# A planner's transfer latency, a row split of one load, and one planner dependency in an attention–mixing–FFN kernel

## Chip, cores and metric

The kernel runs on one core of a Trainium2 chip. The metric is device time in microseconds (us) of one launch; each time shown is of one execution, and results are medians of several.

## What is computed

For each of 8 batches with 8 heads, 576 positions and head size 64, two attentions are added: one over positions averaged by four, whose output is repeated four times, and one over the neighbours at a distance under four. The result, with the heads side by side as 512 channels, goes through a low-rank mixing of positions and a two-layer network.

```python
out_d = sm_attn(q_d, k_d, v_d)                 # q, k, v averaged over 4 positions
out_up = np.repeat(out_d, factor, axis=2)
mask = np.abs(pos[:, None] - pos[None, :]) < factor
...
out_local = np.matmul(attn, v)                 # softmax over the masked scores
x = out_up + out_local                         # then transposed to (B, S, H * D)
h = x.transpose(0, 2, 1) @ U @ V               # U: 576 x 32, V: 32 x 576
u = x + h.transpose(0, 2, 1)
out = u + np.maximum(u @ w_ch1, 0.0) @ w_ch2   # 512 -> 2048 -> 512
```

## The kernel before

Work is cut into **pairs** of heads: four pairs in each batch, numbered 0 to 31 over all batches. Batch 0 is pairs 0 to 3, batch 1 is pairs 4 to 7, batch 2 starts with pair 8. The first five pairs (`NE = 5`) use an early form that needs little from GpSimd; the others use a late form:

- `late_global` loads q and k transposed (`gq`, `gT`) and v (`vr`), averages them on POOL (L415, L417, L510, L512), makes scores on PE (L719, L726, tile `ps_b`), takes the softmax on DVE and ACT, transposes on PE (`ps_t`, L539), multiplies with v (`ps_a`, L552), and scales into `od` on DVE (L556). Two stores of `od` write the repeated output to `up_s` in DRAM, four DMAs a pair (L561). The local scores go through DRAM too (`s_s`, L751, read back into `sc`, L757).
- `local_attn` loads a window of v (`vl`, L708, one buffer) and `up_s` (`ul`, L786). Five times, ACT copies a part of `ul` into a tile `Pt` (L792), POOL fills the rest of `Pt` with products (L798, the last one half as long), and DVE sums it into `acc` (L803). `acc` is stored to `x_s` in DRAM (L805).
- `mix_part` reads `x_s` twice: into `xL` (116 partitions of 5 positions each, two DMAs, L821 and L823, one buffer) and into `Y` (L830). ACT rounds `xL` to `xH` (L836), POOL leaves the remainder in `xL` (L837), PE multiplies both by U (`ps_hu`, L845, ten matmuls in the trace), ACT and DVE form `stk`, PE multiplies by V (`ps_u`, L860, once for each half of the positions), DVE adds to the transposed x (L863), ACT rounds to `uH` (L866), and POOL leaves the remainder in `uL` (L868).

The matrix U comes in through the load `ur` (L372) and a conversion (DVE L342 to L349, ACT L351, POOL L354, tile `Ust`); the same conversion makes `W1H`, `W1L`, `W2H` and `W2L`.

The network works on half a batch, 288 positions, at a time, in 16 steps. A step has a **layer-1 group** of 12 matmuls into `ps_h` (L885) and a **layer-2 group** of 12 into the four `acc` tiles (L908), three steps behind. So batch 0 has 32 layer-1 groups and 32 layer-2 groups, and group 33 is the first of batch 1; it needs `uH` and `uL` of all of pairs 4 to 7. There are two buffers of `uH` and of `uL`. After the last layer-2 group of a half, POOL's `o` (L918, uH + uL) and DVE's sum (L921) give the output, stored by L924.

What decides the order is a **planner** (`Plan.run`). Each operation is recorded with an engine, an assumed duration, the tiles it reads and writes, and a priority: ten times the pair's number, plus 0 for `late_global`, 1 for `local_attn`, 2 for `mix_part`, with small offsets. The planner plays the program through with those durations and latencies, takes the ready operation with the lowest priority on each engine, and writes out a fixed order for PE, DVE, ACT, POOL and SP (all DMAs are issued from SP, in order). On the chip each engine runs its list strictly in that order and waits where an input is missing. The latency of a DMA is `lat` plus an extra for late priorities:

```python
late = (3.0 if r else 4.0) * (prio >= 50)
```

Priority 50 is pair 5. The same list of reads also makes planner dependencies: the name `"UL"` stands for the remainder half of the converted U.

Of the kernel before, what the change touches and what calls it, by code (L numbers as in the profile page):

```python
# [11 lines left out]
F32 = mybir.dt.float32  # L12
# [189 lines left out]
def attn_mix_ffn_kernel(ctx: ExitStack, tc, q, kp, vp, qT, kT, v, U, Ub, V, w1, w2, mask, band, eye, pat, pool, vw, vn, ident, outT):  # L202
    nc = tc.nc
    B, H, S, D = q.shape
# [6 lines left out]
    NFC = w1.shape[0]  # L211
# [4 lines left out]
    R = V.shape[0] // 4  # L216
    MP, MJ = U.shape[0], U.shape[1] // R
# [38 lines left out]
        return two  # L256

    def dma(fn, r, w, prio, kb=295.0, issue=0.47, lat=1.3):
        late = (3.0 if r else 4.0) * (prio >= 50)
        return op(SP, issue, fn, r, w, prio, move=0.01 + kb / 290.0, at=AT if prio >= 35 else 0.0, lat=lat + late)  # L260

    def dve(n, fn, r, w, prio, two_x=False):
# [57 lines left out]
    for _ in range(2):  # L320
        m = kept_tile([NS, 2, KW], "ms_b")
        op(POOL, 0.4, lambda m=m: nc.gpsimd.tensor_copy(
            out=m()[:, :, :, KL:KW].rearrange("p r h k -> p (r h) k"),
# [491 lines left out]
    def mix_part(b, hp, x_s, prio):  # L815
        xL = buf(mix, [MP, 2, MJ, D], F32R, "xL")
        xH = buf(mix, [MP, 2, MJ, D], F32R, "xH")

        def load():
            n = (MP - 1) * MJ  # L820
            nc.sync.dma_start(out=xL().bitcast(F32)[0:MP - 1],  # L821
                              in_=x_s()[:, 0:n, :].rearrange("h (p j) d -> p h j d", j=MJ))
            nc.sync.dma_start(out=xL().bitcast(F32)[MP - 1:MP], in_=x_s()[:, S - MJ:S, :].unsqueeze(0))  # L823
        dma(load, [(x_s, 0), (x_s, 1)], [xL], prio, 295, 1.0, 3.0)
        Y = buf(mix, [128, S // 32, 32], F32, "Y")

        def load_y():
            for hh in range(2):
                for g in range(2):
                    nc.sync.dma_start(  # L830
                        out=Y()[hh * 64 + g * 32:hh * 64 + g * 32 + 32],
                        in_=x_s()[hh, :, g * 32:(g + 1) * 32].rearrange("(a p) d -> p a d", p=32))
        dma(load_y, [(x_s, 0), (x_s, 1)], [Y], prio, 540, 3.6, 0.9)
        xT = buf(mix, [128, S], F32, "xT", bufs=HP)
        dve(576, lambda: nc.vector.transpose(xT(), Y().rearrange("p a d -> p (a d)")), [Y], [(xT, t) for t in range(NT)], prio)
        act(640, lambda: nc.scalar.activation(xH(), xL().bitcast(F32), AF.Copy), [xL], [xH], prio, 0.1)  # L836
        pool_tt(640, lambda: nc.gpsimd.tensor_tensor(  # L837
            out=xL(), in0=xL().bitcast(F32), in1=xH().bitcast(F32), op=ALU.subtract), [xL, xH], [xL], prio)
        ph = psum(ps_m, "ps_hu", "m:x", 2)
        pv = lambda: ph()[:2 * R, :2 * D].rearrange("p (h d) -> p h d", h=2)  # L840

        def hu():
            for i, xx in enumerate((xH, xL)):
                for j in range(MJ):
                    nc.tensor.matmul(pv(), Ust[:, j, :], xx()[:, :, j, :],  # L845
                                     start=(i == 0 and j == 0), stop=(i == 1 and j == MJ - 1))
        op(PE, 0.6, hu, [xH, xL, "UH", "UL"], [ph], prio)
        stk = buf(mix, [128, 2, D], F32R, "stk", bufs=2)
        act(128, lambda: nc.scalar.activation(stk()[0:2 * R], pv(), AF.Copy), [ph], [(stk, 0)], prio, 0.05)
        dve(128, lambda: nc.vector.tensor_tensor(  # L850
            out=stk()[2 * R:3 * R], in0=pv()[0:R], in1=stk()[0:R].bitcast(F32), op=ALU.subtract),
            [ph, (stk, 0)], [(stk, 1)], prio)
        act(128, lambda: nc.scalar.activation(stk()[3 * R:4 * R], pv()[0:R], AF.Copy), [ph], [(stk, 2)], prio, 0.05)
        for t in range(NT):
            tsl = slice(t * TN, (t + 1) * TN)
            pu = psum(ps_m, "ps_u", "m:x", 2)

            def um(tsl=tsl, pu=pu):
                lt = stk().rearrange("p h d -> p (h d)")
                nc.tensor.matmul(pu()[:, :TN], lt, Vst[:, tsl], start=True, stop=True)  # L860
            op(PE, 0.14, um, [(stk, 0), (stk, 1), (stk, 2), "V0H", "V1H", "V0L", "V1L"], [pu], prio)
            uf, ufk = (lambda tsl=tsl: xT()[:, tsl]), (xT, t)
            dve(TN, lambda pu=pu, uf=uf: nc.vector.tensor_tensor(  # L863
                out=uf(), in0=pu()[:, :TN], in1=uf(), op=ALU.add), [pu, ufk], [ufk], prio)
            uH, uL = u_of(b, t)
            act(TN, lambda uH=uH, uf=uf: nc.scalar.activation(uH()[:, hp, :], uf(), AF.Copy),  # L866
                [ufk], [(uH, hp)], prio, 0.1)
            pool_tt(TN, lambda uH=uH, uL=uL, uf=uf: nc.gpsimd.tensor_tensor(  # L868
                out=uL()[:, hp, :], in0=uf(), in1=uH()[:, hp, :].bitcast(F32), op=ALU.subtract),
                [ufk, (uH, hp)], [(uL, hp)], prio)  # L870

    hbuf, accs, last_h = {}, {}, {}
    FIRST, FILL = -10.0, 1000.0
# [23 lines left out]
    def ffn2(s, i):  # L897
        b, t, fc = s
        hH, hL = hbuf.pop(s)
        if fc == 0:  # L900
            accs[(b, t)] = [psum(ps_acc, f"acc{e}", f"acc{e}", 1) for e in range(NDC)]
        ac = accs[(b, t)]

        for e in range(NDC):
            def mm(e=e):
                es = slice(e * 128, (e + 1) * 128)
                for n, (w, hx) in enumerate((("H", hH), ("H", hL), ("L", hH))):
                    nc.tensor.matmul(ac[e]()[:, :TN], W2[w][:, fc, es], hx(),  # L908
                                     start=(fc == 0 and n == 0), stop=(fc == NFC - 1 and n == 2))
            op(PE, PF, mm, [hH, hL, f"W2_{fc}H", f"W2_{fc}L"], [ac[e]], FILL + i + LAG - 0.5)  # L910
        if fc == NFC - 1:
            uH, uL = u_of(b, t)
            for e in range(NDC):
                if e == NDC - 1:
                    o1 = buf(loc, [128, TN], F32, "o1", "o1b", 1)
                else:
                    o1 = buf(ffn, [128, CN], F32, "o1", "cT:o1", 3)
                pool_tt(TN, lambda e=e, o1=o1: nc.gpsimd.tensor_tensor(  # L918
                    out=o1()[:, :TN], in0=uH()[:, e, :].bitcast(F32), in1=uL()[:, e, :].bitcast(F32), op=ALU.add),
                    [(uH, e), (uL, e), f"W2_{NFC - 1}L", "UL"], [o1], FIRST, after=[last_h[i - 1]])  # L920
                dve(TN, lambda e=e, o1=o1: nc.vector.tensor_tensor(  # L921
                    out=o1()[:, :TN], in0=ac[e]()[:, :TN], in1=o1()[:, :TN], op=ALU.add),
                    [ac[e], o1], [o1], FIRST)
                dma(lambda e=e, o1=o1: nc.sync.dma_start(  # L924
                    out=outT[e * 128:(e + 1) * 128, b * S + t * TN:b * S + (t + 1) * TN], in_=o1()[:, :TN]),
                    [o1], [], FIRST, 150, lat=0.4)
# [121 lines left out]
```

## Time and profile before

| what | us |
|---|---|
| median of 3 runs (lowest, highest) | 1049.62 (1048.61, 1051.37) |
| profiled execution, whole | 1052.02 |
| profiled execution, span from first to last instruction | 1050.2 |
| POOL busy in the span | 555.1 |
| DVE busy | 532.0 |
| ACT busy | 390.4 |

The profiled execution stands 1.8 us above its own span and 2.4 us above the median of the runs. PE, ACT and the other names are engines; a granted clock of 1.00 is full speed of TensorE. In a timeline row the first two numbers are start and duration in us, and a bracket tells how long the engine stood idle before and what released it. In a row of the chain of waits, start and length come first. A row of windows gives busy us (and instructions) of PE, PE's weight loads, DVE, ACT and POOL, then the granted clock, the busy share of 16 DMA engines and GB/s.

### The profile page before, as it was taken

The numbers are of one execution on the slowest core, as the hardware profiler recorded it, in microseconds if no ns is written. First come the engines' busy times: TensorE is split into PE (matmuls) and PEld (weight loads), VectorE is DVE, ScalarE is ACT, GpSimd is POOL, SyncE is SP. The second block draws the span as 40 slices with busy tenths as digits, with TensorE's granted clock in tenths as the row PEclk, the third lists the DMA queues.
The fourth block names the chain that finished last, engine by engine and source line by source line (L and its number), as shares of the span: only waits on it lengthen the run. The fifth ranks groups of instructions, "written<-read, shape, count | busy, mean of one in ns | idle before, by whom it ended". The sixth has DMA issues, their size and how long they took to land.

```text
span 1050.2 us, 26946 instructions
## 1 busy us (share of the span) xinstructions
PE 1003.7 (96%) x10831; PEld 980.7 (93%) x10831; DVE 532.0 (51%) x1054; ACT 390.4 (37%) x1234; POOL 555.1 (53%) x567
## 2 busy tenths in 40 slices
PE   6878888979999999999999999999999999999998
PEld 5667887979999999999999999999999999999998
DVE  5887898664454444545464445543553554211121
ACT  3666555333344434343344234433443232111110
POOL 4745467677665756556565826773565715211010
PEclk9888999988999999999999999999999999999999
DMA  9755854455454554553556246633555242100000
GB/s 278 221 157 167 217 169 119 104 135 132 118 125 116 123 136 119 140 119 98 129 147 128 78 123 141 151 93 85 128 131 124 63 102 59 32 1 24 1 24 23
DMA packets 222248, 120.29 MB, mean 115 GB/s; under 512 B 175128, under 2 KB 198092, under 8 KB 222124
## 3 DMA queue, kind: packets, MB, share of 16 engines
q1 hardware_dynamic: 222124, 118.58, 44.8%
q8 instruction: 85, 1.39, 0.6%
q14 instruction: 39, 0.32, 0.1%
HBM read 87.78 MB, written 30.75 MB: 113 GB/s over the span
## 4 chain that ended last, share of the span: by engine, by line
PE 87%; DVE 5%; DMA 3%; ACT 2%; issue 1%; SPq 1%; POOL 0%; DVEq 0%; ACTq 0%
PE acc L908 37%; PE ps_h L885 36%; PE ps_a L552 2%; PE ps_b L719 2%; PE ps_hu L845 2%; DMA w2r<-in_W 1%; PE ps_b L726 1%; PE ps_t L539 1%; PE ps_a L484 1%; DVE c L347 1%; PE ps_v L431 1%; DVE c L349 1%; DVE c L342 1%; PE ps_u L860 1%; DMA s_s<-se 1%
## 5 line engine op out<-in xcount | busy, mean ns | idle before, releaser
L893 DVE SCALAR_TENSOR_TENSOR hL<-ps_h,hH 128x288 fp32r<-128x288 f32 x256 | 116.4, 455 | 384.5 <-ACT hH L892 384.0
L908 PE MATMUL acc<-hH,W2H 128*128 128x288 f32 x1024 | 309.2, 302 | 0.1
L885 PE MATMUL ps_h<-uH,W1H 128*128 128x288 f32 x1024 | 304.7, 298 | 3.7 <-DVE hL L893 2.4
L908 PE MATMUL acc<-hH,W2L 128*128 128x288 f32 x1024 | 302.6, 295 | 2.9 <-POOL W2L L354 2.9
L885 PE MATMUL ps_h<-uL,W1H 128*128 128x288 f32 x1024 | 303.6, 297 | 0.0
L885 PE MATMUL ps_h<-uH,W1L 128*128 128x288 f32 x1024 | 302.3, 295 | 0.0
L908 PE MATMUL acc<-hL,W2H 128*128 128x288 f32 x1024 | 301.8, 295 | 0.0
L798 POOL TENSOR_TENSOR Pt<-vl,at 128x896 f32<-128x896 f32 (+1 forms) x135 | 232.4, 1804 | 106.4 <-DVE acc L803 59.2
L892 ACT ACTIVATE hH<-ps_h 128x288 fp32r<-128x288 f32 x256 | 104.8, 409 | 423.1 <-PE ps_h L885 422.7
L885 PEld LDWEIGHTS ps_h<-uH,W1H 128*128 128x128 f32 x1024 | 193.9, 189 | 4.3 <-DVE hL L893 2.6
L908 PEld LDWEIGHTS acc<-hH,W2L 128*128 128x128 f32 x1024 | 192.4, 188 | 4.0 <-POOL W2L L354 3.9
L885 PEld LDWEIGHTS ps_h<-uH,W1L 128*128 128x128 f32 x1024 | 194.1, 190 | 0.0
L885 PEld LDWEIGHTS ps_h<-uL,W1H 128*128 128x128 f32 x1024 | 193.9, 189 | 0.0
L908 PEld LDWEIGHTS acc<-hH,W2H 128*128 128x128 f32 x1024 | 192.5, 188 | 1.3
L908 PEld LDWEIGHTS acc<-hL,W2H 128*128 128x128 f32 x1024 | 192.7, 188 | 0.0
L803 DVE TENSOR_REDUCE acc<-Pt 128x128 f32<-128x1024 f32 (+1 forms) x135 | 144.6, 1103 | 6.5 <-ACT Pt L792 4.3
L868 POOL TENSOR_TENSOR uL<-xT,uH 128x288 fp32r<-128x288 f32 x56 | 44.2, 812 | 79.9 <-ACT uH L866 72.9
L837 POOL TENSOR_TENSOR xL<-xL,xH 116x640 fp32r<-116x640 f32 x28 | 44.0, 1572 | 69.3 <-ACT xH L836 69.3
L918 POOL TENSOR_TENSOR o<-uH,uL 128x288 f32<-128x288 f32 x64 | 49.8, 818 | 54.3 <-DMA out_t<-o 54.3
L510 POOL TENSOR_TENSOR vr<-vr 72x256 f32<-72x256 f32 x54 | 41.5, 769 | 53.8 <-DMA vr<-in_v 53.8
L792 ACT ACTIVATE Pt<-ul 128x128 f32<-128x128 f32 (+1 forms) x135 | 48.6, 442 | 28.6 <-DVE acc L803 20.5
L743 ACT ACTIVATE se<-ps_b 96x114 f32<-96x114 f32 x108 | 38.4, 356 | 49.8 <-PE ps_b L719 36.0
(129 smaller groups left out, 1122.4 us busy)
## 6 DMA issues: line engine op xcount, KB each, us to landing
vl<-in_vp SPq DMA_DIRECT2D x54, 240.0 KB
out_t<-o SPq DMA_DIRECT2D x64, 144.0 KB
w1r<-in_W SPq DMA_DIRECT2D x16, 512.0 KB
w2r<-in_W SPq DMA_DIRECT2D x16, 512.0 KB
Y<-x_s SPq DMA_DIRECT2D x112, 72.0 KB
xL<-x_s SPq DMA_DIRECT2D x28, 287.5 KB
gT<-in_kT SPq DMA_DIRECT2D x27, 291.0 KB
gq<-in_qT SPq DMA_DIRECT2D x27, 288.0 KB
```

The source lines that it names most:

```text
L510: pool_tt(256, lambda x=x: nc.gpsimd.tensor_tensor(out=x()[:, :, 0:2, :], in0=x()[:, :, 0:2, :], in1=x()[:, :, 2:4, :], op=ALU.add), [x], ...
L743: act(n * KL, lambda p=ps[hh], se=se, n=n, rows=rows: nc.scalar.activation(se()[rows, 0:n].rearrange("p r k -> p (r k)"), p()[rows, 0:n * ...
L792: act(n * D, lambda n=n, ps=ps, Pt=Pt: nc.scalar.activation(Pt()[:, :n, :, 7], ul()[:, ps, :], AF.Copy), [ul], [(Pt, 1)], prio, 0.16)
L798: nc.gpsimd.tensor_tensor(out=Pt()[:, :n, :, 0:7].rearrange("p s d o -> p o s d"), in0=win, in1=at()[:, ps, :].rearrange("p s o -> p o s") ...
L803: dve(8.5 * n * D, lambda n=n, ps=ps, Pt=Pt: nc.vector.tensor_reduce(out=acc()[:, ps, :], in_=Pt()[:, :n], axis=AX.X, op=ALU.add), [(Pt, 0 ...
L837: pool_tt(640, lambda: nc.gpsimd.tensor_tensor(out=xL(), in0=xL().bitcast(F32), in1=xH().bitcast(F32), op=ALU.subtract), [xL, xH], [xL], prio)
L868: pool_tt(TN, lambda uH=uH, uL=uL, uf=uf: nc.gpsimd.tensor_tensor(out=uL()[:, hp, :], in0=uf(), in1=uH()[:, hp, :].bitcast(F32), op=ALU.su ...
L885: nc.tensor.matmul(ps()[:, :TN], w[:, dc, fs], u()[:, dc, :], start=(n == 0), stop=(n == 3 * NDC - 1))
L892: last_h[i] = act(TN, lambda: nc.scalar.activation(hH(), ps()[:, :TN], AF.Relu), [ps], [hH], FIRST, 0.05)
L893: dve(TN, lambda: nc.vector.scalar_tensor_tensor(hL(), ps()[:, :TN], 0.0, hH().bitcast(F32), op0=ALU.max, op1=ALU.subtract), [ps, hH], [hL ...
L908: nc.tensor.matmul(ac[e]()[:, :TN], W2[w][:, fc, es], hx(), start=(fc == 0 and n == 0), stop=(fc == NFC - 1 and n == 2))
L918: pool_tt(TN, lambda e=e, o1=o1: nc.gpsimd.tensor_tensor(out=o1()[:, :TN], in0=uH()[:, e, :].bitcast(F32), in1=uL()[:, e, :].bitcast(F32), ...
```

## The change

There are three edits. The planner's extra latency of a DMA becomes half of what it was for priorities from 50 to under 80 (1.5 or 2.0 us), and stays as it was from 80 on: pairs 5 to 7 fall under it, and of pair 8 the operations with priorities just under 80 (its score stores and the load of `sc`). The load of `xL` is cut at row 112 in place of row 115: one DMA brings 112 rows, the second brings 4 rows, whose positions overlap by one with their neighbours; the host's layout of U puts zeros where a position is held twice, so that U @ x stays the same. The first `o` of an output no longer depends in the plan on `"UL"`.

```diff
--- before.py
+++ after.py
@@ -256,7 +256,7 @@
         return two
 
     def dma(fn, r, w, prio, kb=295.0, issue=0.47, lat=1.3):
-        late = (3.0 if r else 4.0) * (prio >= 50)
+        late = (3.0 if r else 4.0) * (0.5 * (prio >= 50) + 0.5 * (prio >= 80))
         return op(SP, issue, fn, r, w, prio, move=0.01 + kb / 290.0, at=AT if prio >= 35 else 0.0, lat=lat + late)
 
     def dve(n, fn, r, w, prio, two_x=False):
@@ -817,10 +817,12 @@
         xH = buf(mix, [MP, 2, MJ, D], F32R, "xH")
 
         def load():
-            n = (MP - 1) * MJ
-            nc.sync.dma_start(out=xL().bitcast(F32)[0:MP - 1],
-                              in_=x_s()[:, 0:n, :].rearrange("h (p j) d -> p h j d", j=MJ))
-            nc.sync.dma_start(out=xL().bitcast(F32)[MP - 1:MP], in_=x_s()[:, S - MJ:S, :].unsqueeze(0))
+            n = MP - 4
+            nc.sync.dma_start(out=xL().bitcast(F32)[0:n],
+                              in_=x_s()[:, 0:n * MJ, :].rearrange("h (p j) d -> p h j d", j=MJ))
+            t = x_s()[0, n * MJ - 1:n * MJ, :]
+            nc.sync.dma_start(out=xL().bitcast(F32)[n:MP].rearrange("p h j d -> p h (j d)"), in_=bass.AP(
+                tensor=t.tensor, offset=t.offset, ap=[[(MJ - 1) * D, 4], [S * D, 2], [1, MJ * D]]))
         dma(load, [(x_s, 0), (x_s, 1)], [xL], prio, 295, 1.0, 3.0)
         Y = buf(mix, [128, S // 32, 32], F32, "Y")
 
@@ -917,7 +919,7 @@
                     o1 = buf(ffn, [128, CN], F32, "o1", "cT:o1", 3)
                 pool_tt(TN, lambda e=e, o1=o1: nc.gpsimd.tensor_tensor(
                     out=o1()[:, :TN], in0=uH()[:, e, :].bitcast(F32), in1=uL()[:, e, :].bitcast(F32), op=ALU.add),
-                    [(uH, e), (uL, e), f"W2_{NFC - 1}L", "UL"], [o1], FIRST, after=[last_h[i - 1]])
+                    [(uH, e), (uL, e), f"W2_{NFC - 1}L"], [o1], FIRST, after=[last_h[i - 1]])
                 dve(TN, lambda e=e, o1=o1: nc.vector.tensor_tensor(
                     out=o1()[:, :TN], in0=ac[e]()[:, :TN], in1=o1()[:, :TN], op=ALU.add),
                     [ac[e], o1], [o1], FIRST)
@@ -993,9 +995,9 @@
     R = moe_U.shape[1]
     MP, MJ = 116, 5
     pad = [(0, 0), (0, 0), (3, 3), (0, 0)]
-    Up = np.zeros((MP * MJ, R), moe_U.dtype)
-    Up[:S - 1] = moe_U[:S - 1]
-    Up[MP * MJ - 1] = moe_U[S - 1]
+    Up = np.zeros((MP, MJ, R), moe_U.dtype)
+    Up[:112] = moe_U[:560].reshape(112, MJ, R)
+    Up[112:, 1:] = moe_U[560:].reshape(4, MJ - 1, R)
     pos = (np.arange(128) % 64)[:, None, None] * 9 + np.arange(9)[None, :, None]
     tgt = pos + np.arange(7)[None, None, :] - 3
     mask = np.where((tgt >= 0) & (tgt < S), 0.0, -1e9).astype(np.float32)
```

From line 827 on, a line of the changed kernel has a number that is higher by 2 (L845 becomes L847).

The edits to the plan's numbers give another order on each engine. **The end of batch 0.** On PE, before, the matmuls with U for pair 7 (`ps_hu`) stand behind the last `acc` matmul of batch 0, and behind them come pair 9's `ps_a`, pair 7's two `ps_u` and pair 10's scores:

```order
L908 MATMUL acc_2676<-hL,W2H 128x288
L908 MATMUL acc_2676<-hH,W2L 128x288
L845 MATMUL ps_hu<-xH,Ust 64x128 x5
L845 MATMUL ps_hu<-xL,Ust 64x128 x5
L552 MATMUL ps_a<-vs,E 72x64 x8
L860 MATMUL ps_u<-Vst,stk 128x288 x2
L726 MATMUL ps_b<-smk,smq 32x144 x4
L726 MATMUL ps_b<-smk,smq 8x144 x2
```

After, they stand 18 `acc` matmuls before that end (between the second and the third `acc` tile of a group); 12 `acc` matmuls, the two `ps_u` and 6 `acc` matmuls follow, and then layer-1 group 33:

```order
L910 MATMUL acc_2685<-hL,W2H 128x288
L910 MATMUL acc_2685<-hH,W2L 128x288
L847 MATMUL ps_hu<-xH,Ust 64x128 x5
L847 MATMUL ps_hu<-xL,Ust 64x128 x5
L910 MATMUL acc_2693<-hH,W2H 128x288
L910 MATMUL acc_2693<-hL,W2H 128x288
L910 MATMUL acc_2693<-hH,W2L 128x288
```

Pair 9's `ps_a` and pair 10's scores moved to the front: `ps_a` to 9 `acc` matmuls behind pair 6's `ps_hu`, the scores to behind layer-2 group 28. The transposes `ps_t` of pair 10 moved from behind group 35 of layer 1 to behind its group 32. Pair 6's `ps_hu` moved from three quarters through layer-2 group 28 to behind group 26, one layer-1 group earlier too; pair 4's moved from behind layer-2 group 16 to behind group 15.

On POOL, before, the remainder of pair 7 (the one `xL` row) stands behind the last of four `o` (tile uH + uL of batch 0's second half), four `uL` and pair 8's five products:

```order
L918 TENSOR_TENSOR o_3361<-uH,uL 128x288
L868 TENSOR_TENSOR uL<-xT,uH 128x288 x4
L798 TENSOR_TENSOR Pt<-vl,at 128x7x128 x4
L798 TENSOR_TENSOR Pt<-vl,at 128x7x64
L837 TENSOR_TENSOR xL<-xL,xH 116x640
L510 TENSOR_TENSOR vr<-vr 72x2x128
L415 TENSOR_TENSOR gh<-gq 128x288
L512 TENSOR_TENSOR vs<-vr 72x128
L417 TENSOR_TENSOR smq<-gh 128x144
L415 TENSOR_TENSOR gh<-gT 128x288
L417 TENSOR_TENSOR smk<-gh 128x144
L868 TENSOR_TENSOR uL<-xT,uH 128x288 x2
```

After, it stands behind the first two of pair 8's products and the four `o`. The rows ahead of this piece are pair 6's `xL` and the averaging of pair 10's q and k (`gh`, `smq`, `gh`), which stood behind pair 7's `xL` before:

```order
L417 TENSOR_TENSOR smk<-gh 128x144
L870 TENSOR_TENSOR uL<-xT,uH 128x288
L798 TENSOR_TENSOR Pt<-vl,at 128x7x128 x2
L920 TENSOR_TENSOR o_3467<-uH,uL 128x288
L920 TENSOR_TENSOR o_3478<-uH,uL 128x288
L920 TENSOR_TENSOR o_3498<-uH,uL 128x288
L920 TENSOR_TENSOR o_3506<-uH,uL 128x288
L839 TENSOR_TENSOR xL<-xL,xH 116x640
L870 TENSOR_TENSOR uL<-xT,uH 128x288 x3
L798 TENSOR_TENSOR Pt<-vl,at 128x7x128 x2
L870 TENSOR_TENSOR uL<-xT,uH 128x288 x2
L798 TENSOR_TENSOR Pt<-vl,at 128x7x64
```

Three of pair 8's products moved behind pair 7's remainder; two of them still stand ahead of pair 7's first `uL` (the row with x2).

**The load of pair 7's xL.** On SP, before, from pair 8's `ul` to the load of `xL` and `Y` for pair 7:

```order
L786 DMA ul<-up_s 128x576
L569 DMA gq<-in_qT 128x576
L708 DMA vl<-in_vp 64x960 x2
L569 DMA gT<-in_kT 128x582
L805 DMA x_s<-acc 128x576
L508 DMA vr<-in_v 72x2x256
L757 DMA sc<-s_s 128x9x7
L821 DMA xL<-x_s 115x2x320
L823 DMA xL<-x_s 1x2x320
L830 DMA Y<-x_s 32x18x32 x4
```

After, from pair 8's `ul` to the same loads:

```order
L786 DMA ul<-up_s 128x576
L708 DMA vl<-in_vp 64x960 x2
L805 DMA x_s<-acc 128x576
L508 DMA vr<-in_v 72x2x256
L561 DMA up_s<-od 288x1x64 x4
L821 DMA xL<-x_s 112x2x320
L824 DMA xL<-x_s 4x2x320
L832 DMA Y<-x_s 32x18x32 x4
```

Pair 10's loads of `gq` and `gT` and pair 8's of `sc` moved ahead of this piece, and pair 9's four stores of `up_s` now stand ahead of pair 7's `xL`; before, they stood behind pair 7's `Y` and pair 8's `x_s`.

**The load of U.** On SP, before, from a load of W2 to a load for pair 9:

```order
L397 DMA w2r<-in_W 128x1024
L372 DMA ur<-in_U 116x320
L508 DMA vr<-in_v 72x2x256
L561 DMA up_s<-od 288x1x64 x4
L569 DMA gq<-in_qT 128x576
```

After, the same stretch:

```order
L508 DMA vr<-in_v 72x2x256
L397 DMA w2r<-in_W 128x1024
L561 DMA up_s<-od 288x1x64 x4
L372 DMA ur<-in_U 116x320
L569 DMA gq<-in_qT 128x576
```

Pair 7's four stores of `up_s` moved ahead of the load of U (`ur`), and so did one load of `vr`. On POOL the four `o` of batch 0's first half stand directly behind `Ust` in the new order; before, one product stood between.

## Prediction

> **What bounds the kernel now.** I read the page first, then the windows, and then the engines' rows in the one stretch where the windows show PE idle late.
>
> ```profile
> span 1050.2 us, 26946 instructions
> ...
> PE 1003.7 (96%) x10831; PEld 980.7 (93%) x10831; DVE 532.0 (51%) x1054; ACT 390.4 (37%) x1234; POOL 555.1 (53%) x567
> ```
>
> ```profile
> 228.00:236.00 8.00, 1.00 (x8) 0.79 (x8) 6.96 (x10) 1.32 (x3) 8.00 (x7) 0.68 0.44 109
> 236.00:248.40 12.40, 12.23 (x158) 10.92 (x158) 3.36 (x9) 5.37 (x21) 10.96 (x13) 0.65 0.59 141
> 248.40:1042.00 793.60, 793.60 (x8138) 787.78 (x8136) 342.08 (x701) 265.42 (x860) 398.50 (x410) 1.00 0.40 97
> ```
>
> From 248.4 on PE never stops until the tail: 793.60 busy of 793.60 us, at full clock. So the end is set by the time at which PE begins batch 1, and only what happens before that can be gained or lost, unless the new order makes waits behind it. From 228 to 236 PE works 1.00 of 8 us, and then runs at a granted clock of 0.65. This is where batch 0 has ended and batch 1 cannot begin:
>
> ```profile
> 227.74 0.29 PE L908 MATMUL acc<-hH,W2L 128*128 128x288 f32 x1
> 232.33 0.79 PE L845 MATMUL ps_hu<-xH,Ust 116*64 116x128 f32 x5 [4.30 <-ACT xH L836]
> 235.82 0.79 PE L845 MATMUL ps_hu<-xL,Ust 116*64 116x128 f32 x5 [2.70 <-POOL xL L837]
> ```
>
> PE waits for pair 7, the last of batch 1: 4.30 us for xH, 2.70 us for the remainder xL. The chain of waits in this stretch gives the prices of PE's work, at full clock (all rows but the last) and behind the wait (last row):
>
> ```profile
> 200.26 1.03 PE ps_a L552 x16
> ...
> 202.81 1.58 PE ps_h L885 x12
> ...
> 205.71 1.79 PE acc L908 x12
> ...
> 210.28 0.50 PE ps_t L539 x8
> ...
> 217.18 0.60 PE ps_hu L845 x10
> ...
> 219.80 0.27 PE ps_u L860 x2
> 220.07 1.60 PE acc L908 x12
> ...
> 242.42 5.96 PE ps_h L885 x36
> ```
>
> From 228.03 (227.74 + 0.29) to 248.38 (242.42 + 5.96) PE did one ps_hu (0.60), one ps_a (1.03), two ps_u (0.27), one set of scores (205.71 less 204.39, the end of the 1.58 row: 1.32) and three layer-1 groups (3 x 1.58 = 4.74): 7.96 us at full clock, in 20.35. **The place costs 12.4 us**: 7.0 of waiting and 5.4 of low clock behind it.
>
> Why was pair 7 late? ACT and POOL:
>
> ```profile
> 210.17 0.24 ACT L528 ACTIVATE rr<-rs 72x4 f32<-72x4 f32 x1
> ...
> 229.82 0.43 ACT L792 ACTIVATE Pt<-ul 128x128 f32<-128x128 f32 x1 [3.26 <-DVE acc L803]
> ...
> 231.55 0.72 ACT L836 ACTIVATE xH<-xL 116x640 fp32r<-116x640 f32 x1
> ```
>
> ```profile
> 202.94 0.82 POOL L868 TENSOR_TENSOR uL<-xT,uH 128x288 fp32r<-128x288 f32 x1 [5.43 <-ACT uH L866]
> ...
> 213.96 1.57 POOL L837 TENSOR_TENSOR xL<-xL,xH 116x640 fp32r<-116x640 f32 x1 [1.35 <-ACT xH L836]
> ...
> 215.92 3.09 POOL L918 TENSOR_TENSOR o<-uH,uL 128x288 f32<-128x288 f32 x4
> 221.18 0.80 POOL L868 TENSOR_TENSOR uL<-xT,uH 128x288 fp32r<-128x288 f32 x1 [2.18 <-ACT uH L866]
> 224.11 2.34 POOL L868 TENSOR_TENSOR uL<-xT,uH 128x288 fp32r<-128x288 f32 x3 [2.12 <-ACT uH L866]
> 226.41 7.93 POOL L798 TENSOR_TENSOR Pt<-vl,at 128x896 f32<-128x896 f32 x5
> ...
> 240.16 1.57 POOL L868 TENSOR_TENSOR uL<-xT,uH 128x288 fp32r<-128x288 f32 x2 [1.04 <-ACT uH L866]
> ```
>
> Pair 7's xH stands on ACT behind copies for pair 8 that wait for DVE, and its remainder stands on POOL behind all five products of pair 8, 7.93 us of work that batch 1 does not need. It is a matter of order.
>
> **The change part by part.** *The halved latency* moves pair 7 forward in the lists. I count from H, the start of pair 6's ps_hu. Before, H is 217.18. In the new order it stands 21 acc matmuls (1.60 / 12 = 0.133 each) and one layer-1 group earlier: 2.8 + 1.58 = 4.4, so H = 212.8. Its input can follow: pair 5's ps_hu moves two layer-1 groups and 18 acc matmuls ahead (3.16 + 2.4) and has one ps_a, one set of scores and one ps_t more before it (2.85), so 2.7 earlier; pair 5's uL, for which POOL stood idle 5.43 us at 202.94, pair 7's products behind it, and pair 6's remainder behind those move along: 213.96 + 1.57 less 2.7 = 212.8, just in time.
>
> From H on, PE has: ps_hu 0.60, 9 acc 1.2, ps_a 1.03, ps_u 0.13, 3 acc 0.4, a layer-1 group 1.58, ps_u 0.13, a layer-2 group 1.6, scores 1.32 (H + 8.0), then two layer-1 groups, one layer-2 group, ps_t 0.5 and 18 acc (H + 15.7), pair 7's ps_hu 0.6, 12 acc 1.6, two ps_u 0.27, 6 acc 0.8: **PE is at group 33 at H + 18.9.**
>
> POOL, from H on: pair 6's uL begins 1.4 behind its ps_u (221.18 less 219.80), so at H + 4.2, ends at H + 5.0; two products of pair 8 (7.93 over 4.6 whole ones: 1.75 each) H + 8.5; four o, 3.09, H + 11.6. Then pair 7's remainder, which needs xH. On ACT xH stands right behind rr of the softmax of pair 10, whose scores end at H + 8.0; before, from the scores' end (205.71) to rr's end (210.41) went 4.7, so rr ends at H + 12.7, xH at H + 13.4. So the remainder runs from H + 13.4 to H + 15.0, three uL (2.34) to 17.3, two more products (3.5) to 20.8, pair 7's first uL to H + 21.6. **Group 33 can start at H + 21.6 = 234.4**, 2.7 behind PE. What is late next is thus POOL, with two products of pair 8 still ahead of pair 7's uL.
>
> Before, it started at 242.42: 8.0 us gained. Pair 10's ps_t is now done ahead of it: 0.5. The three groups took 5.96 at low clock; at full clock they take 4.74, 1.2 less. But a wait of this length has been seen to cost clock:
>
> ```profile
> 114.95 0.61 PE L885 MATMUL ps_h<-uH,W1H 128*128 128x288 f32 x1 [2.36 <-DVE hL L893]
> ...
> 117.76 0.44 PE L885 MATMUL ps_h<-uH,W1L 128*128 128x288 f32 x1
> ```
>
> Behind 2.36 us of waiting twelve matmuls took from 114.95 to 118.0, 3.05 in place of 1.58. So the groups are worth between -0.2 and +1.2; I take 0.5. Sum of this place: **9.0 us**. The Trainium skill, "TensorE: Matmul & The Clock Gate" (What's actually happening), says that the clock falls to half after an idle window of about 3.4 us; by it a wait of 2.7 would cost only itself, and the sum would be 9.7. This trace disagrees: 2.36 us were enough.
>
> *Ahead of it*, pair 4's ps_hu and the scores of pairs 7 and 8 stand earlier on PE. Rows of PE's waits and of POOL:
>
> ```profile
> PE ps_b L726 <- DVE od L556: 2.8, 2, 2.0
> ...
> PE ps_hu L845 <- ACT nb L522: 2.6, 1, 2.6
> ```
>
> ```profile
> 167.45 1.33 POOL L354 TENSOR_TENSOR W2L<-c,W2H 128x512 fp32r<-128x512 f32 x1
> 169.41 0.54 POOL L354 TENSOR_TENSOR Ust<-cu,Ust 116x160 fp32r<-116x160 f32 x1 [0.63 <-ACT Ust L351]
> ```
>
> The two waits (2.0 and 2.6) hang on slots that the scores and ps_a share; both get more work between. At best 4.6 us go, at worst none, since layer-2 group 16 cannot start before the last W2 remainder (168.8) and pair 4's ps_hu not before Ust (169.95) in either order. Pair 6 follows on time only as far as POOL does; I take 1.5, nearer the lower end because of Ust.
>
> *The 112-row load.* Alone on the queues, a load of xL shows:
>
> ```profile
> 588.60:591.80 3.20, 3.20 (x27) 3.20 (x26) 0.46 (x1) 0.41 (x1) 3.20 (x3) 1.00 0.29 92
> ```
>
> At 92 GB/s and 0.29 of 16 engines (4.6 engines) its 287.5 KB take 3.2 us. If 112 rows use all of them, it is 3.2 x 4.6 / 16 = 0.9; if not, nothing changes: 0 to 2.3 us on each load. The Trainium skill, "DMA: Bandwidth & Descriptors" (Why a DMA increments its semaphore by 16 and not by 1), gives the largest divisor up to 16 of the slowest dimension as the number of engines: 5 for 115 rows, 16 for 112, 4 for 4 rows. By that rule it is the 0.9; the row agrees on the 5. For pair 7 the load stands on SP behind four stores of up_s:
>
> ```profile
> 223.84 0.28 SPq L821 DMA_DIRECT2D xL<-x_s  x1
> ...
> 239.25 3.40 SPq L561 DMA_DIRECT2D up_s<-od  x4
> ```
>
> The stores wait for od of pair 9, which comes 0.5 behind ps_a (H + 2.8): H + 3.4, 3.4 for issuing, so xL is issued at about H + 6.9 and has moved by H + 12.0 even at 3.2 us and a start up to 1.9 us behind its issue. ACT is at xH at H + 12.7. So I take 0 for this edit: it is cover, worth up to 2 us if the stores come late. *The freed first o* stands directly behind Ust in the new order all the same: 0, and it could only move it by one product, 1.75.
>
> Behind 248.4 the plan's latencies are as before (0 taken; a new wait would cost its length, a gain isn't possible where PE is never idle). Sum: 9.0 + 1.5 = 10.5. The profiled execution, 1052.0, would become 1041.5; it stood 2.4 above the median, so from the median **1049.6 less 10.5 is 1039**.
>
> **Rivals.** *POOL stays late in part (chance 0.17).* POOL has the same work up to pair 7's first uL, less one half product (1.1), which ended at 240.98; that it ends at 234.4 rests on idle time that goes: 5.43, 2.18, 2.12 and 1.35 in its rows above. If half of these 11 us go, the uL ends at 240.98 - 1.1 - 5.5 = 234.4, as forecast; if a quarter, at 237 to 238, the wait is long enough for the low clock, and 4 to 6 us are gained: 1043 to 1046. For it: POOL is busy 8.00 of 8.00 in the bad window. Against: DVE and ACT are not.
>
> *The order moves and the wait only changes its name (0.15).* If none of POOL's idle time goes, the gain is 1.1 + 0.5 and what of 1.5 arrives: 1046.5 to 1052.5. This is also the case in which the change does not do what it says. Against it: xH no longer waits for pair 8's sums, and 4.4 us of PE's work moved behind H.
>
> *The load of U holds everything (0.09), slower.* In the new order the load of U stands on SP behind pair 7's four stores.
>
> ```profile
> 157.83 0.28 SPq L372 DMA_DIRECT2D ur<-in_U  x1
> ...
> 163.00 3.31 SPq L561 DMA_DIRECT2D up_s<-od  x4
> ```
>
> ```profile
> 161.55 0.35 ACT L341 ACTIVATE cu<-ur 116x160 f32<-116x160 f32 x1
> ```
>
> ```profile
> 164.70 0.23 DVE L342 TENSOR_SCALAR cu<-cu 116x160 f32<-116x160 f32 x1
> ```
>
> Were the stores no earlier than before, U would be loaded at 166.4, 8.6 later; 164.70 less 161.90 is 2.8 of slack, so DVE, with the last W2 conversion queued behind cu, would stop 5.8 us, and PE's layer-2 group 16 with it. It is slower than before from the point where this eats the gain at batch 0's end: stores later than about 166, or these 5.8 together with a gain of under 2.5, which gives 1053 to 1056. Against it: od of pair 7 hangs on ps_a, which moved from behind layer-2 group 13 to behind group 11.
>
> *More goes (0.08).* The 2.7 us wait vanishes too, and all of the 4.6: 10.7 + 0.5 + 1.2 + 4.6 = 17.0, 1033 to 1036.
>
> **How the numbers follow.** The forecast, 1036 to 1043, has 0.51. The range leaves out the upper half of no change, the slower case and a part of the best: 1034 to 1047. A measurement of this kernel tells about 0.3% (3.1 us) from no change. Faster by more: 0.51 + 0.17 + 0.08 = 0.76; within: 0.15; slower: 0.09.
>
> **What would show it.** Pair 7's ps_hu without a wait over 1 us, the last wait before the long full stretch on a layer-1 matmul with POOL uL as releaser, of 1 to 4 us; group 33 near 233; Ust near 170; xL loads that hold the DMA engines about 1 us. Wrong would be: a wait of pair 6's or 7's ps_hu of over 4 us, DVE idle at cu, or PE idle anywhere behind 250.

## The result, and the profile after

| | median us (lowest to highest, runs) | profiled execution, its span |
|---|---|---|
| before | 1050.1 (1048.61 to 1051.37, 6) | 1052.02, 1050.2 |
| changed | 1039.22 (1036.51 to 1040.1, 6) | 1039.02, 1037.2 |

The medians are 10.9 us apart. The ratio of the runs is 0.9891 with a 95% interval of 0.9875 to 0.9907, that is 9.8 to 13.1 us less.

The first part of the page, and then a view of windows on both sides of the moment from which PE no longer stops:

```profile
span 1037.2 us, 26946 instructions
...
PE 998.7 (96%) x10831; PEld 977.2 (94%) x10831; DVE 527.7 (51%) x1054; ACT 387.5 (37%) x1234; POOL 556.0 (54%) x567
```

```profile
228.89:236.30 7.41, 5.49 (x40) 5.03 (x39) 5.90 (x12) 2.85 (x8) 7.25 (x11) 1.00 0.57 147
236.30:1029.00 792.70, 792.70 (x8130) 786.94 (x8129) 341.15 (x698) 261.60 (x855) 401.97 (x410) 1.00 0.40 97
```

The long full stretch, which began at 248.4, begins at 236.3 and is as full as before. Ahead of it PE idles 1.92 us of 7.41, at a granted clock of 1.00 where it was 0.65. PE's rows at that place, from the timeline:

```profile
228.89 0.29 PE L887 MATMUL ps_h<-uH,W1H 128*128 128x288 f32 x1
...
230.09 0.29 PE L887 MATMUL ps_h<-uH,W1H 128*128 128x288 f32 x1
231.51 0.40 PE L887 MATMUL ps_h<-uL,W1H 128*128 128x288 f32 x1 [1.14 <-POOL uL L870]
...
234.42 0.40 PE L887 MATMUL ps_h<-uH,W1H 128*128 128x288 f32 x1 [0.78 <-DVE hL L895]
```

The waits for pair 7's xH and xL (4.30 and 2.70) are gone. Group 33 begins at 228.89, directly behind batch 0's last layer-2 group, and ten of its twelve matmuls run before one needs `uL` of pair 7. POOL's rows for the same stretch:

```profile
199.88 8.47 POOL L798 TENSOR_TENSOR Pt<-vl,at 128x896 f32<-128x896 f32 x5 [1.39 <-DMA vl<-in_vp]
208.17 1.59 POOL L839 TENSOR_TENSOR xL<-xL,xH 116x640 fp32r<-116x640 f32 x1
213.98 0.80 POOL L870 TENSOR_TENSOR uL<-xT,uH 128x288 fp32r<-128x288 f32 x1 [0.85 <-ACT uH L868]
214.74 3.69 POOL L798 TENSOR_TENSOR Pt<-vl,at 128x896 f32<-128x896 f32 x2
218.27 3.10 POOL L920 TENSOR_TENSOR o<-uH,uL 128x288 f32<-128x288 f32 x4
223.19 1.58 POOL L839 TENSOR_TENSOR xL<-xL,xH 116x640 fp32r<-116x640 f32 x1 [1.81 <-DMA s_s<-se]
224.72 2.33 POOL L870 TENSOR_TENSOR uL<-xT,uH 128x288 fp32r<-128x288 f32 x3
227.01 3.80 POOL L798 TENSOR_TENSOR Pt<-vl,at 128x896 f32<-128x896 f32 x2
230.65 1.57 POOL L870 TENSOR_TENSOR uL<-xT,uH 128x288 fp32r<-128x288 f32 x2
```

Five products of pair 7, pair 6's remainder (208.17), two products of pair 8, the four `o`, pair 7's remainder (223.19), two more products of pair 8, and batch 1's last `uL`, whose first half ends at about 231.4 and lets PE go on at 231.51. The 1.81 us in front of pair 7's remainder stand beside `s_s` in this view, but they end with ACT's `xH` of pair 7 (222.38 to 223.10), and in a second execution of the same kernel the same wait (1.79) stands beside ACT `xH`.

**How one execution can be read.** Single executions differ early, whatever the change. The changed kernel, the same again, and three kernels of the experiments that are alike up to pair 5's load had pair 4's `ps_hu` at 167.25, 169.70, 172.12, 167.53 and 167.34. So the runs are compared by medians, and the traces by stretches that begin late enough: the time from the first matmul of layer-1 group 19 to that of group 36. It is 76.0 us before (174.3 to 250.3), and 66.4 and 66.5 in two executions of the changed kernel. That is 9.5 to 9.6 us, nearly all of the difference of the medians. The two profiled executions are 13.0 apart, and 3.1 of that stand ahead of group 19 (174.3, 171.3); the five executions above reach group 19 at anything from 171.3 to 176.2, so these 3.1 can't be told from chance.

### The profile page after: what moved, and what is told of

Read it like the earlier page. It is cut to its first block, busy times and chain, and to the rows that moved or that the text cites. A ratio compares the mean times of both kernels' runs of the same rounds, so it can differ in the third digit from the quotient of the medians.

```text
span 1037.2 us, 26946 instructions
## 1 busy us (share of the span) xinstructions
PE 998.7 (96%) x10831; PEld 977.2 (94%) x10831; DVE 527.7 (51%) x1054; ACT 387.5 (37%) x1234; POOL 556.0 (54%) x567
## 4 chain that ended last, share of the span: by engine, by line
PE 86%; DVE 6%; DMA 2%; ACT 2%; POOL 1%; SPq 1%; issue 1%; DVEq 0%; ACTq 0%
PE acc L910 37%; PE ps_h L887 36%; PE ps_a L552 2%; PE ps_b L719 2%; PE ps_hu L847 2%; DVE c L347 1%; PE ps_t L539 1%; PE ps_b L726 1%; PE ps_a L484 1%; DVE c L342 1%; DVE c L349 1%; DMA w2r<-in_W 1%; DVE c L344 1%; PE ps_v L431 1%; PE ps_u L862 1%
```

## The experiments

Ratios are to runs of the kernel before on the same chip.

| kernel | median us (lowest to highest, runs) | ratio, 95% | group 19 to 36 |
|---|---|---|---|
| latency alone | 1046.0 (1043.91 to 1048.54, 6) | 0.9944, 0.9922 to 0.9965 | 70.5 |
| load alone | 1049.71 (1047.2 to 1054.73, 12) | 0.9986, 0.9967 to 1.0004 | 75.4 |
| changed, old load | 1044.89 (1042.31 to 1048.12, 6) | 0.9931, 0.9909 to 0.9953 | 70.3 |
| changed, o tied | 1040.02 (1038.25 to 1042.69, 6) | 0.9886, 0.9864 to 0.9908 | 66.4 |
| changed, old latency | 1044.81 (1043.54 to 1046.34, 6) | 0.9941, 0.9923 to 0.9959 | 72.0 |
| pair 5's load slow | 1044.43 (1039.79 to 1047.39, 8) | 0.9940, 0.9916 to 0.9964 | 69.7 |
| pair 6's load slow | 1040.01 (1036.62 to 1043.37, 6) | 0.9902, 0.9876 to 0.9928 | 66.1 |
| pair 7's load slow | 1041.38 (1039.22 to 1042.79, 6) | 0.9916, 0.9890 to 0.9942 | 67.5 |
| U ahead of W2 chunk 14 | 1038.1 (1036.6 to 1044.17, 6) | 0.9899, 0.9868 to 0.9929 | not comparable |
| changed, once more | 1041.21 (1039.18 to 1042.51, 6) | 0.9906, 0.9886 to 0.9925 | 66.5 |
| a quarter of the latency | 1037.71 (1034.71 to 1042.16, 6) | 0.9879, 0.9855 to 0.9903 | 63.7 |
| a quarter, and U early | 1037.08 (1034.18 to 1038.86, 5) | 0.9859, 0.9836 to 0.9881 | not comparable |

In the two marked ones pair 4's `ps_hu` stands elsewhere against group 19.

### One edit alone, or all but one

**The latency alone**: the kernel before with

```diff
-        late = (3.0 if r else 4.0) * (prio >= 50)
+        late = (3.0 if r else 4.0) * (0.5 * (prio >= 50) + 0.5 * (prio >= 80))
```

> The kernel before with the halved latency alone. Theory: the order does it all, so 1039 to 1040 (10 to 11 us less than before), pair 7's ps_hu without a wait, and the last wait before the full stretch on a layer-1 matmul for POOL uL, 1 to 2 us. Rival 1, the 112-row load carries part of it (5.0 us less on two loads, or 2.3 on one, in the chain ps_a, store, load, xH, xL, uL): 1041.5 to 1044. Rival 2, the freed first o carries part: 1040.5 to 1042, by one product of 1.75 us on POOL.

It gave 0.9944, about half of the gain, less than theory or either rival allowed. Pair 7's `ps_hu` has no wait, as the theory said, but PE has a wait of 1.64 us for pair 6's `xL` and one of 2.03 for `uL` in group 33.

**The load alone**: the kernel before with the pieces of the diff for `load()` and for the host's `Up`.

> The kernel before with the 112-row load alone; the order of every engine stays that of before. Theory: xH of pair 7 stands on ACT behind copies for pair 8, so a load that lands sooner is not used: 0 us, 1049.5 to 1050.5, and the 4.30 us wait for xH stays. Rival 1: pair 7's xH comes sooner by up to 2.3 us, 1047.5 to 1048.5.

The interval holds 1.0, and pair 7's waits stay (4.36 and 2.92 us). In the old order the load alone brings nothing that these runs can tell from zero.

**The changed kernel with the old load**:

```diff
-            n = MP - 4
+            n = (MP - 1) * MJ
...
-    Up = np.zeros((MP, MJ, R), moe_U.dtype)
+    Up = np.zeros((MP * MJ, R), moe_U.dtype)
```

> The changed kernel with the old load of 115 rows and 1 row; same order on every engine but for the pieces of the loads. Theory: 0 to 0.5 us slower than the changed kernel, since ACT comes to xH of pair 7 only behind rr of pair 10 (222.27) and the load issued at 216.9 has moved by then even in 3.2 us. Rival 1: the load ends after ACT is free, 1 to 2.3 us more of waiting for POOL uL in front of the 11th matmul of group 33: 1040.5 to 1042, and with the low clock behind the wait up to 1043.5.

The theory fell: without the load 2.6 to 4.2 us of the gain are gone by the ratios (0.9931 against 0.9906 and 0.9891), and 3.9 in the stretch (70.3 against 66.4); its interval lies clear of the first measurement's and overlaps the second's. The rival's wait is not what brings it: PE waits 1.45 us for `uL` in group 33, against 1.14. PE's waits behind 165 us in this kernel (in all, times, longest), with a window behind the second of them:

```profile
PE ps_hu L845 <- POOL Ust L354: 2.5, 1, 2.5
PE ps_hu L845 <- POOL xL L837: 2.0, 1, 2.0
PE ps_h L885 <- POOL uL L868: 1.5, 1, 1.5
PE ps_h L885 <- DVE hL L893: 0.8, 1, 0.8
```

```profile
213.60:216.60 3.00, 3.00 (x16) 3.00 (x17) 2.48 (x6) 1.85 (x7) 2.84 (x6) 0.50 0.89 264
```

The second row is new: pair **6**'s `ps_hu` waits 1.98 us for its remainder, and PE then works at half clock, 16 matmuls in 3 us. On POOL that remainder stands behind the five products of pair 7, and these had waited for the load of pair 7's values:

```profile
203.75 8.39 POOL L798 TENSOR_TENSOR Pt<-vl,at 128x896 f32<-128x896 f32 x5 [2.83 <-DMA vl<-in_vp]
211.99 1.55 POOL L837 TENSOR_TENSOR xL<-xL,xH 116x640 fp32r<-116x640 f32 x1
```

SP's queue tells why that load was late. First the changed kernel, then the one with the old load; each from pair 5's load on:

```profile
185.32 0.47 SPq L821 DMA_DIRECT2D xL<-x_s  x1
...
186.25 2.04 SPq L832 DMA_DIRECT2D Y<-x_s  x4
188.39 3.28 SPq L751 DMA_DIRECT2D s_s<-se  x4
...
194.17 1.17 SPq L708 DMA_DIRECT2D vl<-in_vp  x2
```

```profile
186.61 0.42 SPq L821 DMA_DIRECT2D xL<-x_s  x1
...
187.73 3.76 SPq L830 DMA_DIRECT2D Y<-x_s  x4
191.59 3.14 SPq L751 DMA_DIRECT2D s_s<-se  x4
...
197.22 1.18 SPq L708 DMA_DIRECT2D vl<-in_vp  x2
```

The four `Y` loads right behind the slow load took 3.76 us to issue in place of 2.04, nearly all of it in the fourth (2.22 in place of 0.61), and `vl` followed 10.6 us behind the load in place of 8.9 (197.22 - 186.61, 194.17 - 185.32). Then the products begin late, pair 6's remainder, and PE.

**The changed kernel with the first o tied to `"UL"` again**:

```diff
-                    [(uH, e), (uL, e), f"W2_{NFC - 1}L"], [o1], FIRST, after=[last_h[i - 1]])
+                    [(uH, e), (uL, e), f"W2_{NFC - 1}L", "UL"], [o1], FIRST, after=[last_h[i - 1]])
```

> The changed kernel with the first o tied to U's remainder again. In the order two products of POOL change places with the four o, and three places of PE by a layer-2 group at most. Theory: within 1 us of the changed kernel (1038.2 to 1040.2), as the wait for POOL uL of pair 7 keeps its producers in the same order. Rival 2: 1.75 us more, 1041, since pair 5's uL and all behind it come one product later.

No difference can be seen: 0.9886 against 0.9891, 66.4 us from group 19 to 36 in both, and PE's waits behind 165 us are those of the changed kernel (2.5 for Ust, 1.2 for `uL`, 0.8 for `hL`).

### Which pair's load it is

The changed kernel, with the 112 rows of one pair's load in two pieces, of 92 and 20 rows, so that it is slow again; shown for pair 5 (batch 1, second pair). The order of every engine is that of the changed kernel.

```diff
-            nc.sync.dma_start(out=xL().bitcast(F32)[0:n],
-                              in_=x_s()[:, 0:n * MJ, :].rearrange("h (p j) d -> p h j d", j=MJ))
+            [nc.sync.dma_start(out=xL().bitcast(F32)[a:z], in_=x_s()[:, a * MJ:z * MJ, :].rearrange("h (p j) d -> p h j d", j=MJ))
+             for a, z in (((0, 92), (92, n)) if (b, hp) == (1, 1) else ((0, n),))]
```

> The changed kernel, with the 112 rows of pair 5's load alone cut into 92 and 20 rows, to make it slow again; the order of every engine stays. Theory now: what the quick load brings is not at pair 7, as the prediction costed it, but at pair 5: with the slow load, the four Y loads behind it take 1.5 to 2 us longer to issue on SP, ACT comes to xH of pair 5 later and waits for the load, and the loads of pair 7's values behind them come late, so POOL's five products of pair 7 and the remainder xL of pair 6 behind them come about 2 us late. So pair 6's ps_hu waits 1 to 2 us for xL and the clock falls: 1042 to 1044.5, and in the profile 4 to 5 us more from the first layer-1 group to group 33. Rival, pair 6's own load or pair 7's: within 1 us of the changed kernel, 1038.5 to 1040.2, no wait at pair 6's ps_hu.

> The same with pair 6's load alone made slow. Theory: POOL comes to pair 6's xL only when its five products end, and its xH has been ready by then (in the changed kernel with the old load at 211.04, POOL free at 212.1); 0 to 0.7 us, 1039 to 1040, with ACT's wait for the load about 1 us. Rival, the own load of pair 6 is on the path: a wait of 1 to 2 us for xL at pair 6's ps_hu, 1042 to 1044.5.

> The same with pair 7's load alone made slow. Theory, and the prediction's step: ACT comes to pair 7's xH behind rr of pair 10, when the load is just there: 0 to 0.5 us more in the wait for POOL uL in front of the 11th matmul of group 33: 1039 to 1040. Rival, the whole of the load's 5 us is here: 1043 to 1044.5, with a wait of 3 us or more for POOL uL and the low clock behind it.

With pair 5's load slow the whole picture is back, at 1044.43; two of the eight runs (1039.79 and 1040.14) were as quick as the changed kernel, and no trace shows why. `Y` takes 3.68 us to issue, and `vl` follows 10.6 us behind the load. SP's queue and ACT's row for pair 5, POOL's timeline, and then PE's row at pair 6's `ps_hu`:

```profile
189.96 0.97 SPq L821 DMA_DIRECT2D xL<-x_s  x2
...
191.32 3.68 SPq L832 DMA_DIRECT2D Y<-x_s  x4
195.10 2.95 SPq L751 DMA_DIRECT2D s_s<-se  x4
...
200.54 1.17 SPq L708 DMA_DIRECT2D vl<-in_vp  x2
```

```profile
196.28 0.74 ACT L838 ACTIVATE xH<-xL 116x640 fp32r<-116x640 f32 x1 [1.37 <-DMA xL<-x_s]
```

```profile
206.72 8.40 POOL L798 TENSOR_TENSOR Pt<-vl,at 128x896 f32<-128x896 f32 x5 [2.56 <-DMA vl<-in_vp]
214.95 1.57 POOL L839 TENSOR_TENSOR xL<-xL,xH 116x640 fp32r<-116x640 f32 x1
```

```profile
216.57 0.72 PE L847 MATMUL ps_hu<-xL,Ust 116*64 116x128 f32 x5 [1.87 <-POOL xL L839]
```

From group 19 to 36 it is 3.3 us more (69.7 less 66.4): 1.87 of waiting, and 1.5 from a clock of 0.52 behind it. With pair 6's load slow nothing is lost, though ACT waits 1.68 us for that load: POOL is not there yet. With pair 7's slow it is 1.1 more, between theory and rival; ACT waits 0.65 us for it, which comes out on PE as

```profile
232.24 0.51 PE L887 MATMUL ps_h<-uL,W1H 128*128 128x288 f32 x1 [1.85 <-POOL uL L870]
```

0.7 us more of waiting than 1.14, and again half clock behind it (0.52 over 3 us); in return the wait of 0.78 for `hL` is gone. The three together make 4.1 (3.3 - 0.3 + 1.1), and the old load in all pairs cost 3.9 in this stretch. With pair 5's load slow `Y` takes 1.6 us longer and `vl` comes 1.7 us later behind the load, so SP's queue accounts for it (0.5 us of issuing is that of the second piece, and the issues in between took a little less). ACT's wait of 1.37 us for the same load is the other way by which it could have come. The rows speak against it: the fourth `Y` had been issued by 195.00, before ACT began `xH` at 196.28, the stores of `s_s` behind it took no longer than in the changed kernel (2.95 and 3.28), and POOL then stood idle 2.56 us for `vl`. No run had the one without the other.

### The old latency with the other two edits

> The changed kernel with the old latency: the 112-row load and the freed first o alone. Theory: the load is worth 4 to 5 us only in the new order, where pair 6 would wait behind it; in the old order pair 7 stands on ACT and POOL behind pair 8 whatever its load does, so both long waits of pair 7's ps_hu stay (about 4.3 and 2.8 us): 1047.5 to 1050. Rival, load and latency simply add: 4 to 6 us less than before, 1044 to 1046.

Here the edit is the first line of the diff undone. The theory fell: 0.9941, as good as the latency alone. The time lies in the rival's range, but not by its sum, since the load alone brought nothing. Of pair 7's two waits the one for `xH` (4.30) is gone and the one for the remainder stays:

```profile
228.41 0.52 PE L847 MATMUL ps_hu<-xL,Ust 116*64 116x128 f32 x5 [3.18 <-POOL xL L839]
```

POOL has, in front of pair 7's remainder,

```profile
218.55 2.00 POOL L798 TENSOR_TENSOR Pt<-vl,at 128x896 f32<-128x896 f32 x1
...
223.30 3.65 POOL L798 TENSOR_TENSOR Pt<-vl,at 128x896 f32<-128x896 f32 x2
226.81 1.55 POOL L839 TENSOR_TENSOR xL<-xL,xH 116x640 fp32r<-116x640 f32 x1
```

three products of pair 8, where it had five. The freed `o` moved the planner's later choices, and so it does in the old order part of what the halved latency does. It is not the load by itself: with the load alone both of pair 7's waits stayed. The freed `o` by itself was not tried, so what it is worth without the load is open.

### Further than the change

**U ahead of W2 chunk 14**, which aims at the 2.50 us in front of pair 4's `ps_hu`:

```diff
     for f in range(NFC):
+        load_u(38) if f == 14 else None
         load_w2(f, W2P + W2S * f)
-    load_u(38)
```

> The changed kernel, with U's load and conversion put ahead of the W2 chunk 14 in place of behind chunk 15 (Ust four products of work earlier on POOL). From pair 8's first ps_t on the order is that of the changed kernel; pair 4's ps_hu stands behind layer-2 group 14. Theory: the wait of 2.50 us for Ust in front of pair 4's ps_hu goes and with it 1.0 us of low clock, and W2's last chunks come 0.5 to 1 us later, which layer-2 group 15 or 16 may wait for; 1.5 to 3 us less, if POOL keeps up for pair 6 and 7: 1036 to 1037.5. Rival: POOL is the bound of this stretch, so the wait only goes over to W2's remainder or to pair 6's xL: 1039 to 1041.

The wait for Ust goes, and a new one of 1.76 us stands at pair 4's `ps_u`, for DVE's `stk`, which neither theory nor rival had named; 1038.1 lies between the two, and the interval doesn't tell it from the changed kernel.

**The changed kernel once more, a quarter of the latency** (`0.25 * (prio >= 50) + 0.75 * (prio >= 80)`), and **a quarter with U early**:

> The changed kernel itself once more, beside the next three on the same chip. Theory: its first 85 us differ from one execution to the next whatever the change (the start of the first layer-1 group stood at 83.2 to 86.9 in four kernels that are alike up to there), so 1038 to 1041 and a ratio that holds 0.9891; in the profile, from layer-1 group 19 to group 36 66.1 to 66.6 us as before. Rival, the change itself made the early part 1.6 us shorter: the first group starts at 84.2 again, within 0.3.

> The changed kernel with a quarter of the late pairs' latency for batch 1 in place of a half. In the order POOL has one product of pair 8 ahead of batch 1's last uL in place of two, and pair 6's ps_hu stands one layer-2 group less 3 matmuls earlier on PE. Theory: the 1.14 us wait for POOL uL in front of group 33's 11th matmul goes, but pair 6's remainder xL, which was just in time behind five products (four and one now), makes PE wait about 1 us at pair 6's ps_hu, with some low clock behind it: 1038 to 1041. Rival, only the wait goes: 1037.5 to 1038.5.

> The changed kernel with a quarter of the latency and with U ahead of W2 chunk 14. Theory: pair 4's wait for Ust only went over to its ps_u in the run with U moved alone, so nothing is added to the run with a quarter alone: 1037 to 1041. Rival, pair 4's earlier uL lets POOL run ahead for pairs 6 and 7, and both waits go: 1035 to 1037.

The same kernel gave 1041.21, just over the range expected, and began its first group at 84.8, between 84.2 and the 85.8 of before: the early difference can't be told from chance. With a quarter the theory fell and its rival held. POOL has a single product in front of the last `uL`:

```profile
229.40 2.05 POOL L798 TENSOR_TENSOR Pt<-vl,at 128x896 f32<-128x896 f32 x1
231.28 3.88 POOL L870 TENSOR_TENSOR uL<-xT,uH 128x288 fp32r<-128x288 f32 x5
```

and group 33 starts at 234.4 without a wait; pair 6's remainder, now behind four products, came in time too. Group 19 to 36 is 2.7 us shorter (63.7); the medians alone, 1037.71 and 1041.21 on the same chip, do not show it, since their intervals overlap. With U early besides, the view of PE's waits from 150 to 250 us has two rows left:

```profile
PE ps_u L862 <- DVE stk L852: 1.8, 1, 1.8
PE acc L910 <- POOL W2L L354: 0.6, 1, 0.6
```

1037.08 against 1041.21 on the same chip, at the low end of the theory's range and just over the rival's; the lowest ratio of all (0.9859), whose interval overlaps with that of a quarter alone. Both beat the kernel before. The intervals of the changed kernel on this chip and of a quarter with U early (0.9886 to 0.9925, 0.9836 to 0.9881) do not overlap; that of the first measurement (0.9875 to 0.9907) overlaps it a little.

## Why the prediction was right, and where it was not

The time, 1039 against 1039.22, was right, and so was the place. That it came within 0.2 us is luck: the same kernel gave 1041.21 in a second measurement, and the first one's profiled execution, put at 1041.5, came at 1039.02. The terms were 9.0 there and 1.5 ahead of it; measured are 9.5 to 9.6 and about 0, so two errors partly cancel. What was wrong is which edit brings it.

- **What bounds.** Right: the gain is the earlier start of the full stretch, and behind it nothing was gained or lost.
- **H, the start of pair 6's `ps_hu`, 4.4 earlier by its place in the order.** From group 19's first matmul to H it is 42.7 us before and 38.0 in the changed kernel: 4.7. Right, but only with the quick load, below.
- **Ahead of it, 1.5.** Mis-sized: about 0. From the first layer-1 matmul to that of group 19 it was 88.6 us before and 87.0 to 89.3 in five executions of the changed order. The scores' wait of 2.0 went, but pair 4's `ps_hu` still waits 2.50 (2.57 before), now for Ust and with a low clock behind it, W2's remainder takes 1.06 (0.78), and a wait of 0.95 for `hL` is new.
- **POOL from H on.** Within 0.5 us at each step: pair 6's `uL` at H + 4.7 (predicted 4.2), `xH` done H + 13.8 (13.4), pair 7's remainder done H + 15.5 (15.0), its first `uL` about H + 22.1 (21.6), with H at 209.32. A product of pair 8 took 1.85 to 1.90 and not 1.75 (the prediction's own 7.93 over 4.6 is 1.72). What is late next was POOL's `uL` of pair 7, as said. PE stood at group 33 at H + 19.6 (18.9).
- **"Group 33 can start at H + 21.6", a shortfall of 2.7.** The step failed: a layer-1 group runs through the four pairs' channels one after another, so ten matmuls, 1.3 us, need nothing of pair 7's remainder. What was left to wait was 1.14; the last wait ahead of the full stretch is another, 0.78 for `hL`.
- **The low clock behind that wait.** It did not come (1.00) behind 1.14 us. For 2.7 the prediction went by the 2.36 us of one row; but in the same trace the wait of 2.57 at pair 4's `ps_hu`, whose row it shows, left the clock at 1.00, which it did not look at. What decides this is in the last section. The place was worth 9.5 to 9.6 in place of 9.0: the shorter wait and the full clock add to it, the wait of 0.78 for `hL` and PE's later arrival at group 33 take from it.
- **The load, 0, "it is cover".** The step that failed most. It is worth 3.9 us in the traces and 2.6 to 4.2 by the ratios. The prediction looked at pair 7 alone, where cover was nearly right (1.1 us at stake, 2 allowed). It took pair 6's remainder to be "just in time" without asking on which load POOL's products ahead of it hang, and so put the load's part down to the latency: the latency alone is worth 0.9944. In the trace of before this could be seen only in part: pair 5's four `Y` issues behind a slow load (185.66, 3.06 us) stand in SP's order ahead of the load of pair 7's values (195.01), but there POOL did not wait for these.
- **The first o, 0.** Right in the new order; in the old one it is worth some 4.7 us on top of the load by the ratios (0.9986 to 0.9941) and 3.4 in the stretch (75.4 to 72.0), by the order that the planner then makes.
- **Rivals.** None of them happened. U was loaded at 155.00 in place of 157.83, so the load of U held nothing.

## What to carry to other kernels

A quicker transfer is not priced by the wait of its own consumer alone. Look at what is issued behind it on the same queue, and follow the latest of those to an engine that waits; a chain that is "just in time" in a sum deserves a second look at every load in it. And where a planner decides the order, edits that look independent can do the same thing, so each should be measured with and without the others.

## What the hardware showed beyond that

**How long a wait costs clock.** In two executions of kernels alike up to there, PE waited 1.73 and 1.70 us at the same layer-1 matmul. The windows behind, first of the changed kernel, then of the one with pair 6's load slow:

```profile
112.18:114.58 2.40, 2.40 (x15) 2.34 (x16) 2.37 (x6) 0.63 (x1) 1.11 (x1) 0.75 0.60 158
```

```profile
111.57:113.97 2.40, 2.40 (x22) 2.38 (x23) 2.37 (x6) 0.88 (x2) 1.11 (x1) 1.00 0.54 129
```

15 matmuls against 22. Of the waits looked at, those of 1.14, 1.64 and 1.70 left the clock at 1.00, those of 1.85, 1.87 and 1.98 brought it to 0.50 to 0.52 for 3 us, which costs 1.5 us more; in between 1.73 lost some and a wait of 1.76 in front of pair 4's `ps_u` none. But length alone does not decide it: in front of pair 4's `ps_hu`, 2.57 us in the kernel before and 2.51 with the latency alone left the clock at 1.00, while 2.50 in the changed kernel halved it. In these traces the granted clock changes only at steps of 3.41 us, or multiples of it, whose place differs from execution to execution. Two neighbouring steps around that wait, before and changed (these rows count PE's matmuls alone, and then give clock, DMA share and GB/s):

```profile
169.50:172.91 3.41, 1.65 (x13) 1.00 0.39 64
172.91:176.32 3.41, 2.60 (x25) 1.00 0.36 107
```

```profile
164.59:168.00 3.41, 0.91 (x13) 1.00 0.19 9
168.00:171.41 3.41, 3.41 (x17) 0.50 0.46 134
```

Before, the wait falls into two steps, with 1.76 and 0.81 us of idle PE; in the changed kernel one step holds all 2.50, and the next has half clock. From 90 to 1000 us the 14 traces hold 26 steps at full clock in which PE idled 1.79 us or more, and each was followed by half clock. Of 44 steps with 1.0 to 1.78 us of it 9 were, of 3590 with less than 1.0 none. So about half of a step is enough, and whether a wait of about 2 us costs clock depends on where it falls in the steps. The Trainium skill, "TensorE: Matmul & The Clock Gate" (What's actually happening), puts the fall behind an idle window of about 3.4 us, which runs free of the kernel; the traces agree on the length of the window and that it runs free, but not that all of it has to be idle: no wait was that long but the one for `xH` of pair 7 in the old order (4.30, and 4.36 with the load alone).

**A load over more DMA engines.** Alone on the queues, a load of 112 rows shows in 0.8 us windows:

```profile
575.60:576.40 0.80, 0.80 (x8) 0.80 (x8) 0.19 (x1) 0.41 (x1) 0.80 (x1) 1.00 0.66 173
576.40:577.20 0.80, 0.80 (x8) 0.80 (x8) 0.27 (x1) 0.00 (x0) 0.80 (x2) 1.00 0.55 198
577.20:578.00 0.80, 0.80 (x8) 0.80 (x8) 0.00 (x0) 0.00 (x0) 0.80 (x1) 1.00 0.00 0
```

1.6 us in place of 3.2, with 0.6 of the engines' time in place of 0.29: half, not the third that the estimate of 0.9 us took. And what is issued behind it is issued faster: over the whole kernel the 112 `Y` loads took 60.8 us to issue, against 93.3 before (2.2 and 3.3 for each four). It goes with the load and not with the order: 64.3 with the load alone, 97.5 in the changed kernel with the old load. The difference lies in the last of each four, 51.1 us in all before and 17.2 in the changed kernel. Why that issue takes long behind a slow load is not shown.
